# Single-token attention with a gated mixer branch: halved PE score sums, collects batched by four, the mixer moved to heads 22 to 24, and a fixed VectorE order

## The chip, the cores and the metric

The kernel runs on one core of one Trainium2 chip. The metric is the device time in microseconds (us). Engines are named as in the profile: PE is TensorE's matmul side, PEld its weight loads, DVE is VectorE, ACT is ScalarE, SP is SyncE, which here only issues DMA transfers.

Ratios are computed as the mean time of one kernel's runs over the mean of the other's runs in the same rounds, so a ratio is not quite the ratio of the medians quoted beside it.

## The reference, cut to what matters

```python
q = (x @ wq).reshape(1, 1, 32, 128)                 # one token, 32 heads of 128
scores = einsum(q, k_cache) * 128 ** -0.5           # k_cache: 32 heads x 16384 x 128, bf16
a = (softmax(scores) @ v_cache).reshape(1, 4096) @ wo
z = gelu(x @ w_in); z1, z2 = z[:896], layernorm(z[896:])
b = (z1 * (w_sp * z2 + b_sp)) @ w_out               # the mixer branch, on the same x
g = sigmoid((x * gate_w).sum())
out = g * a + (1 - g) * b                           # 512 numbers
```

The two caches are 32 heads x 2 x 4 MiB. With the weights they make 279.58 MB, of which every byte is read once and used for almost no arithmetic.

## The kernel before

Per head a k tile and a v tile of 128 x 16384 bf16 are loaded. DVE multiplies k by the broadcast q, in two halves. PE adds up slices of the product with an identity matrix as weights (16 matmuls of 512 columns per half), DVE reduces the 8 partial sums that are left, ACT takes the exponential. The attend uses 32 matmuls with four columns of p as weights, which leave their answer on the diagonal of a 4 x 4 block; ACT copies that out and 4 fp32 matmuls per head collect it.

```python
    def load_k(h):
        t = kv.tile([P, NJ * Dh], BF16, name="k_t", tag="k", bufs=3)
        nc.sync.dma_start(out=t[:], in_=k_src[h])
        ktile[h] = t
    # load_v(h): the same with tag "v", bufs=2
    load_k(0); load_k(1); load_k(2); load_v(0)
    # ... then the loads of w_in and w_out (the mixer's weights) ...

    def scores_half(h, s):
        # ... ks: half s of the k tile, qh: q broadcast over it ...
        nc.vector.tensor_tensor(out=ks, in0=ks, in1=qh, op=ALU.mult)
        s_ps = ps_s.tile([P, NH, W], FP32, name="s_ps")
        for i in range(NS):                       # NS = 16, W = 8
            nc.tensor.matmul(s_ps[:, :, :], lhsT=ident[:, :], rhs=ks[:, :, i * W:(i + 1) * W],
                             start=(i == 0), stop=(i == NS - 1))
        nc.vector.tensor_reduce(out=s_sb[:, s * NH:(s + 1) * NH], in_=s_ps[:, :, :],
                                axis=AX.X, op=ALU.add)
        # ... after the second half: the exponential, on ACT ...

    AHEAD = 2
    with tc.manual_schedule(engines={mybir.EngineType.PE}):   # PE in program order
        # ... scores of heads 0 and 1 ...
        for h in range(H - 1):
            if h > 0:
                # (only while h + AHEAD < H)
                load_k(h + AHEAD)
                load_v(h)
            scores_half(h + AHEAD, 0)
            if 0 < h <= WIDE:
                collect(h - 1)
            if h < WIDE:
                scores_half(h + AHEAD, 1)
                attend_wide(h)
            # ... else: the narrow attend of the last heads ...
            if h == 1:
                gate()
                mixer()          # z = x @ w_in, gelu, layernorm, u, then u @ w_out
```

A k buffer is free again when the sums of its head are done, a v buffer when its attend is done; only then can SP issue the next load into it (in the trace of the kernel before, SP waited 28 times for the matmuls of an attend before a v load, 333.0 us in all).

The softmax here doesn't subtract the row's maximum and nothing guards it: scores larger than these inputs give would overflow.

## Time and profile before

| | before |
|---|---|
| time, median of the first 4 runs | 662.51 us (661.65 to 663.8) |
| span of the profiled run | 662.0 us |
| DMA bytes; share of 16 engines' span | 279.58 MB; 98.5% |
| PE / DVE / ACT busy | 528.9 / 329.8 / 39.5 us |
| rate from 160 to 620 us | 424 to 440 GB/s |

The next lines are from the page of the kernel before: busy times with shares of the span and instruction counts; the DMA queues with packets, MB and share of 16 engines; and two groups of instructions (busy us, mean ns of one | idle time before them and what ended it).

```profile
span 662.0 us, 6195 instructions
PE 528.9 (80%) x2835; PEld 233.8 (35%) x2835; DVE 329.8 (50%) x164; ACT 39.5 (6%) x108; POOL 0.7 (0%) x6
...
q1 hardware_dynamic: 10520, 279.58, 98.5%
q8 instruction: 22, 0.36, 0.2%
...
L222 DVE TENSOR_TENSOR k_t<-k_t,qb 128x8192 bf16<-128x8192 bf16 x64 | 280.5, 4421 | 136.7 <-DMA k_t<-in_A_k_cache_dram 136.7
L225 PE MATMUL s_ps<-k_t,ident 128*128 128x512 bf16 x1024 | 268.9, 423 | 95.0 <-DVE k_t L222 95.0
```

The SP queue, q1, keeps the DMA engines busy 98.5% of the span, and DVE waits 136.7 us in all for k tiles to land: the kernel is limited by its loads, and PE's 80% is not a limit.

The table of stretches shows where the loads are not at their full rate. Its last two columns are the mean busy share of the DMA engines and GB/s.

```profile
120.00:124.00 4.00, 4.00 (x20) 1.61 (x19) 4.00 (x2) 1.69 (x3) 0.00 (x0) 1.00 0.93 401
124.00:128.00 4.00, 4.00 (x20) 1.54 (x18) 4.00 (x2) 0.57 (x1) 0.00 (x0) 1.00 0.58 213
128.00:132.00 4.00, 4.00 (x24) 2.17 (x22) 1.94 (x2) 0.00 (x0) 0.00 (x0) 1.00 0.85 344
132.00:136.00 4.00, 4.00 (x20) 1.63 (x19) 1.01 (x2) 0.29 (x2) 0.00 (x0) 1.00 1.02 442
```

The timeline of SP (start us, us, what) shows the cause, and that of DVE and PE what lies behind it:

```profile
92.11 0.33 SPq L85 DMA_DIRECT2D v_t<-in_A_v_cache_dram  x1
92.54 0.37 SPq L78 DMA_DIRECT2D k_t<-in_A_k_cache_dram  x1
126.89 0.33 SPq L85 DMA_DIRECT2D v_t<-in_A_v_cache_dram  x1
127.31 0.38 SPq L78 DMA_DIRECT2D k_t<-in_A_k_cache_dram  x1
...
98.83 4.42 DVE L222 TENSOR_TENSOR k_t<-k_t,qb 128x8192 bf16<-128x8192 bf16 x1
...
108.70 0.89 PE L207 MATMUL a_ps<-u,w_out 128*128 128x1 bf16 x28 [10.37 <-DVE u L202]
```

No load is issued from 92.5 to 126.9 us. PE, whose order is fixed, stands at the mixer's last matmul and waits 10.37 us for u, which DVE finishes late because two products of 4.4 us were put among the mixer's small steps. So the attend that frees the v buffer comes late, and the queue runs dry.

### The profile page before, as it was taken

How to read it: one execution, taken by the hardware profiler on the slowest of the kernel's cores; microseconds unless marked ns; L12 is line 12 of the kernel's file. 1: busy time of each engine (PE TensorE's matmuls, PEld its weight loads, DVE VectorE, ACT ScalarE, POOL GpSimd, SP SyncE). 2: the span in 40 equal slices, each digit the busy share in tenths (PEclk: the TensorE clock that was granted, in tenths of full speed). 3: DMA queues.
4: the chain of work that ended last, by engine and by line, in shares of the span. 5: the costliest groups of instructions: out<-in, count | busy, mean ns of one | idle time of the engine just before them, and what ended most of it. 6: DMA issues, size and time to landing. Idle time of an engine off the chain costs nothing.

```text
span 662.0 us, 6195 instructions
## 1 busy us (share of the span) xinstructions
PE 528.9 (80%) x2835; PEld 233.8 (35%) x2835; DVE 329.8 (50%) x164; ACT 39.5 (6%) x108; POOL 0.7 (0%) x6
## 2 busy tenths in 40 slices
PE   2777584999879798788799878789878879987884
PEld 0233242444323343333233333234333323333453
DVE  1592515666554445555444556444555544455600
ACT  0200020100000000000000000000000000000000
POOL 0000000000000000000000000000000000000000
PEclk9799595999989989889998988998988999897965
DMA  9999999899999999999999999999999999999995
GB/s 380 436 419 442 422 439 429 356 429 440 427 428 439 422 437 436 423 438 427 432 437 420 437 436 423 438 429 430 435 424 436 433 428 435 432 431 430 431 414 248
DMA packets 10554, 279.98 MB, mean 423 GB/s; under 512 B 1182, under 2 KB 1184, under 8 KB 1568
## 3 DMA queue, kind: packets, MB, share of 16 engines
q1 hardware_dynamic: 10520, 279.58, 98.5%
q8 instruction: 22, 0.36, 0.2%
q14 instruction: 4, 0.03, 0.0%
q10 hardware_dynamic: 8, 0.00, 0.0%
HBM read 279.58 MB, written 0.00 MB: 422 GB/s over the span
## 4 chain that ended last, share of the span: by engine, by line
DMA 60%; PE 30%; DVE 9%; SPq 1%; issue 0%; ACT 0%; DVEq 0%
DMA k_t<-in_A_k_cache_dram 52%; PE s_ps L225 15%; PE d_ps L250 12%; DVE k_t L222 8%; DMA v_t<-in_A_v_cache_dram 4%; DMA wo_t<-in_A_wo_dram 4%; PE o_ps L259 2%; SPq L85 1%; PE o_ps L239 1%; PE z_ps L167 0%; PE a_ps L317 0%; PE a_ps L207 0%; SPq L293 0%; PE tot_ps L184 0%; SPq L69 0%
## 5 line engine op out<-in xcount | busy, mean ns | idle before, releaser
L222 DVE TENSOR_TENSOR k_t<-k_t,qb 128x8192 bf16<-128x8192 bf16 x64 | 280.5, 4421 | 136.7 <-DMA k_t<-in_A_k_cache_dram 136.7
L225 PE MATMUL s_ps<-k_t,ident 128*128 128x512 bf16 x1024 | 268.9, 423 | 95.0 <-DVE k_t L222 95.0
L250 PE MATMUL d_ps<-v_t,p_t 128*4 128x512 bf16 x928 | 205.0, 379 | 0.0
L225 PEld LDWEIGHTS <-ident 128*128 128x128 bf16 x1024 | 105.9, 106 | 243.7 <-issue 148.2
L250 PEld LDWEIGHTS <-p_t 128*4 128x4 bf16 x928 | 76.4, 85 | 126.1 <-issue 12.3
L227 DVE TENSOR_REDUCE s_sb<-s_ps 128x64 f32<-128x512 f32 x64 | 44.2, 690 | 148.4 <-PE s_ps L225 148.4
L231 ACT ACTIVATE p_t<-s_sb 128x128 bf16<-128x128 f32 x32 | 9.9, 309 | 385.4 <-DVE s_sb L227 385.4
L259 PEld LDWEIGHTS o_ps<-ident_f,d_sb 4*128 4x128 f32 x232 | 27.9, 186 | 12.3 <-issue 12.3
L259 PE MATMUL o_ps<-ident_f,d_sb 4*128 4x1 f32 x232 | 30.4, 248 | 0.0
L254 ACT COPY d_sb<-d_ps 4x512 f32<-4x512 f32 x29 | 16.7, 575 | 170.7 <-PE d_ps L250 170.7
L121 PE MATMUL q_ps<-wq_t,xb 128*128 128x512 bf16 x32 | 9.7, 477 | 10.5 <-DMA wq_t<-in_A_wq_dram 10.5
L239 PE MATMUL o_ps<-p_t,v_t 128*128 128x1 bf16 x384 | 10.8, 165 | 4.4 <-DMA v_t<-in_A_v_cache_dram 4.3
L239 PEld LDWEIGHTS <-v_t 128*128 128x128 bf16 x384 | 10.5, 102 | 4.7 <-DMA v_t<-in_A_v_cache_dram 4.7
L121 PEld LDWEIGHTS <-xb 128*128 128x128 bf16 x32 | 3.7, 117 | 16.2 <-issue 13.1
L207 PE MATMUL a_ps<-u,w_out 128*128 128x1 bf16 x28 | 0.9, 165 | 10.4 <-DVE u L202 10.4
L317 PE MATMUL a_ps<-o,wo_t 128*128 128x1 bf16 x128 | 3.9, 166 | 4.2 <-DMA wo_t<-in_A_wo_dram 4.2
L124 DVE CAST qb<-q_ps 128x512 bf16<-128x512 f32 x1 | 0.7, 693 | 11.2 <-PE q_ps L121 11.2
L231 ACT ACTIVATION_READ_ACCUMULATOR p_t<-s_sb 128x1 f32 x32 | 6.0, 186 | 0.0
L304 DVE TENSOR_TENSOR o_sb<-o_ps,rl 128x32 bf16<-128x32 f32 x1 | 0.2, 192 | 10.3 <-PE o_ps L239 10.3
L317 PEld LDWEIGHTS <-wo_t 128*128 128x128 bf16 x128 | 3.6, 104 | 4.5 <-DMA wo_t<-in_A_wo_dram 4.5
L126 ACT CAST qb<-q_ps 128x512 bf16<-128x512 f32 x7 | 4.1, 586 | 15.9 <-PE q_ps L121 15.9
L207 PEld LDWEIGHTS <-w_out 128*128 128x128 bf16 x28 | 1.1, 111 | 10.4 <-issue 10.4
(65 smaller groups left out, 24.9 us busy)
## 6 DMA issues: line engine op xcount, KB each, us to landing
k_t<-in_A_k_cache_dram SPq DMA_DIRECT2D x32, 4096.0 KB, 37.5
v_t<-in_A_v_cache_dram SPq DMA_DIRECT2D x31, 4096.0 KB, 28.9
wq_t<-in_A_wq_dram SPq DMA_DIRECT2D x1, 4096.0 KB, 12.3
v_t<-in_A_v_cache_dram SPq DMA_DIRECT2D x1, 2048.0 KB, 11.1
v_t<-in_A_v_cache_dram SPq DMA_DIRECT2D x2, 1024.0 KB, 14.7
wo_t<-in_A_wo_dram SPq DMA_DIRECT2D x1, 2048.0 KB, 21.1
w_in<-in_B_w_in_dram SPq DMA_DIRECT2D x1, 1792.0 KB, 44.6
wo_t<-in_A_wo_dram SPq DMA_DIRECT2D x1, 1024.0 KB
```

Source lines behind the costliest of these rows:

```text
L85: nc.sync.dma_start(out=t[:, a * Dh:b * Dh], in_=v_src[h][:, a * Dh:b * Dh])
L121: nc.tensor.matmul(q_ps[:, :], lhsT=xb[:, c, :], rhs=wq[:, c, nb * QB:(nb + 1) * QB], start=(c == 0), stop=(c == DC - 1))
L126: nc.scalar.copy(out=qb[:, nb * QB:(nb + 1) * QB], in_=q_ps[:, :])
L222: nc.vector.tensor_tensor(out=ks, in0=ks, in1=qh, op=ALU.mult)
L225: nc.tensor.matmul(s_ps[:, :, :], lhsT=ident[:, :], rhs=ks[:, :, i * W:(i + 1) * W], start=(i == 0), stop=(i == NS - 1))
L227: nc.vector.tensor_reduce(out=s_sb[:, s * NH:(s + 1) * NH], in_=s_ps[:, :, :], axis=AX.X, op=ALU.add)
L231: nc.scalar.activation(out=p_t[:], in_=s_sb[:], func=ACT.Exp, scale=inv_sqrt_dh, accum_out=L_sb[:, h:h + 1])
L239: nc.tensor.matmul(o_ps[:, h:h + 1], lhsT=v3[:, j, :], rhs=p_sb[h][:, j:j + 1], start=(j == 0), stop=(j == NJ - 1))
L250: nc.tensor.matmul(d_ps[:, :], lhsT=p_sb[h][:, g * R:(g + 1) * R], rhs=vtile[h][:, g * R * Dh:(g + 1) * R * Dh], start=(g == 0), stop=(g = ...
L254: nc.scalar.copy(out=d_sb[:], in_=d_ps[:, :])
L259: nc.tensor.matmul(o_ps[:, h:h + 1], lhsT=diag[h][:, r * Dh:(r + 1) * Dh], rhs=ident_f[:, r:r + 1], start=(r == 0), stop=(r == R - 1))
L317: nc.tensor.matmul(a_ps[:, c:c + 1], lhsT=wo4[:, k, c, :], rhs=o2[:, k:k + 1], start=False, stop=(k == H - 1), skip_group_check=True)
```

## The change

Its intent is to take work off PE and to take the mixer out of the critical start. Four things change: (1) from head 3 DVE adds the upper half of each product to the lower one, in bf16, so PE sums 8 slices per half; (2) four heads' attends share one PSUM bank (rows 0, 32, 64, 96), which is drained and collected once; (3) the mixer's loads are issued at head 19 and its work is cut into pieces placed at heads 22 to 24; (4) the order of DVE is fixed too. The gate's sum is taken on 8 partitions by DVE, with one small matmul over them, instead of by eight matmuls.

```diff
-    NS = Dh // W
+    NS = Dh // 2 // W
@@ loads of w_in, w_out, gate_w, w_sp, b_sp: from the start into load_mixer(), called at h == MIX - 3 @@
+    def scores_mult(h):
+        # ... qh as before ...
+        for ks in halves(h):
+            nc.vector.tensor_tensor(out=ks, in0=ks, in1=qh, op=ALU.mult)
+            if h > 2:
+                nc.vector.tensor_tensor(out=ks[:, :, 0:Dh // 2], in0=ks[:, :, 0:Dh // 2],
+                                        in1=ks[:, :, Dh // 2:Dh], op=ALU.add)
+    def scores_sum(h, s):
+        # ...
+        ns = NS if h > 2 else 2 * NS
+    # scores_exp(h): both reduces, then the exponential
@@ attend and collect @@
+    G = 4
-        d_ps = ps_s.tile([R, R * Dh], FP32, name="d_ps")
+        d_ps = d_banks[(h // G) % 2]
+            nc.tensor.matmul(d_ps[32 * g:32 * g + R, :], lhsT=p_sb[h][:, t * R:(t + 1) * R], ...
+                if h % G == G - 1 or h == WIDE - 1:
+                    drain(h - h % G)
+                    due = (h - h % G, h % G + 1)
@@ the loop @@
-    with tc.manual_schedule(engines={mybir.EngineType.PE}):
+    MIX = 22
+    dve_extra = {MIX: [gate_x], MIX + 1: [gate_out, mixer_gelu], MIX + 2: [mixer_norm]}
+    pe_extra = {MIX: [gate_ps, mixer_z], MIX + 1: [mixer_tot], MIX + 2: [mixer_out]}
+    with tc.manual_schedule(engines={mybir.EngineType.PE, mybir.EngineType.DVE}):
-            if h == 1:
-                gate()
-                mixer()
```

More of the change, by code (lines that the diff above doesn't have):

```diff
@@ L60 @@
     x_row = const.tile([1, D], BF16, name="x_row")
-    gw_row = const.tile([1, D], BF16, name="gw_row")
-    wb_row = const.tile([1, 2], BF16, name="wb_row")
     nc.scalar.dma_start(out=x_row[:], in_=A_x.rearrange("b s d -> (b s) d"))
-    nc.scalar.dma_start(out=gw_row[:], in_=gate_w.rearrange("(a d) -> a d", a=1))
-    nc.scalar.dma_start(out=wb_row[:, 0:1], in_=B_w_sp)
-    nc.scalar.dma_start(out=wb_row[:, 1:2], in_=B_b_sp.rearrange("(a d) -> a d", a=1))
     wq_t = kv.tile([P, DC * HDh], BF16, name="wq_t", tag="v")
@@ L100 @@
     load_v(0)
-    w_in = const.tile([P, DC, F], BF16, name="w_in")
-    nc.sync.dma_start(out=w_in[:].rearrange("p c f -> p (c f)"),
-                      in_=B_w_in.rearrange("(p c) f -> p (c f)", c=DC))
-    w_out = const.tile([P, FhC, D], BF16, name="w_out")
-    nc.sync.dma_start(out=w_out[:].rearrange("p k n -> p (k n)"),
-                      in_=B_w_out.rearrange("(p k) n -> p (k n)", k=FhC))
     xb_ps = ps_m.tile([P, DC * P], FP32, name="xb_ps", tag="mm")
@@ L132 @@
                               in_=ident[0:H, 0:H])
-    ident_f = const.tile([4, 4], FP32, name="ident_f")
-    nc.vector.tensor_copy(out=ident_f[:], in_=ident[0:4, 0:4])
+    pick = const.tile([P, 4, 4], FP32, name="pick")
+    nc.vector.tensor_copy(out=pick[:].rearrange("p r g -> p g r"),
+                          in_=ident[:].rearrange("p (g m) -> p g m", m=32)[:, :, 0:4])
+    d_banks = [ps_1.tile([P, 512], FP32, name=f"d_ps{i}") for i in range(2)]
+    for t in d_banks:
+        nc.vector.memset(t[:, :], 0.0)
     a_ps = ps_1.tile([P, 512], FP32, name="a_ps")
@@ L141 @@
     wbf = const.tile([P, 2], FP32, name="wbf")
-    def gate():
-        gw_ps = ps_m.tile([P, DC + 2], FP32, name="gw_ps", tag="mm")
-        for c in range(DC):
-            nc.tensor.matmul(gw_ps[:, c:c + 1], lhsT=gw_row[0:1, c::DC], rhs=ones_row[0:1, 0:1],
-                             start=True, stop=True)
-        nc.tensor.matmul(gw_ps[:, DC:DC + 2], lhsT=ones_row[0:1, :], rhs=wb_row[0:1, :],
-                         start=True, stop=True)
-        gw_col = const.tile([P, DC], BF16, name="gw_col")
-        nc.vector.tensor_copy(out=gw_col[:], in_=gw_ps[:, 0:DC])
-        nc.vector.tensor_copy(out=wbf[:], in_=gw_ps[:, DC:DC + 2])
-        g_ps = ps_m.tile([P, 1], FP32, name="g_ps", tag="mm")
-        for c in range(DC):
-            nc.tensor.matmul(g_ps[:, :], lhsT=xb[:, c, :], rhs=gw_col[:, c:c + 1],
-                             start=(c == 0), stop=(c == DC - 1))
-        nc.scalar.activation(out=g_sb[:], in_=g_ps[:, :], func=ACT.Sigmoid)
-        nc.scalar.activation(out=gm_sb[:], in_=g_ps[:, :], func=ACT.Sigmoid, scale=-1.0)
@@ L162, in mixer, with load_mixer @@
-    def mixer():
+    w_in = const.tile([P, DC, F], BF16, name="w_in")
+    w_out = const.tile([P, FhC, D], BF16, name="w_out")
+    xg = const.tile([8, 2, D // 8], BF16, name="xg")
+    wb_row = const.tile([1, 2], BF16, name="wb_row")
+    def load_mixer():
+        nc.sync.dma_start(out=w_in[:].rearrange("p c f -> p (c f)"),
+                          in_=B_w_in.rearrange("(p c) f -> p (c f)", c=DC))
+        nc.sync.dma_start(out=xg[:, 0, :], in_=A_x.rearrange("b s (p d) -> (b s p) d", p=8))
+        nc.sync.dma_start(out=xg[:, 1, :], in_=gate_w.rearrange("(p d) -> p d", p=8))
+        nc.sync.dma_start(out=wb_row[:, 0:1], in_=B_w_sp)
+        nc.sync.dma_start(out=wb_row[:, 1:2], in_=B_b_sp.rearrange("(a d) -> a d", a=1))
+        nc.sync.dma_start(out=w_out[:].rearrange("p k n -> p (k n)"),
+                          in_=B_w_out.rearrange("(p k) n -> p (k n)", k=FhC))
@@ new lines, with gate_x, gate_ps @@
+    branch = {}
+    def gate_x():
+        xgp = const.tile([8, D // 8], BF16, name="xgp")
+        nc.vector.tensor_mul(out=xgp[:], in0=xg[:, 0, :], in1=xg[:, 1, :])
+        xgs = const.tile([8, 1], FP32, name="xgs")
+        nc.vector.reduce_sum(out=xgs[:], in_=xgp[:], axis=AX.X)
+        branch["xgs"] = xgs
+    def gate_ps():
+        xgs = branch["xgs"]
+        g_ps = ps_m.tile([P, 3], FP32, name="g_ps", tag="mm")
+        nc.tensor.matmul(g_ps[:, 0:1], lhsT=ones_f[0:8, :], rhs=xgs[:, :], start=True, stop=True)
+        nc.tensor.matmul(g_ps[:, 1:3], lhsT=ones_row[0:1, :], rhs=wb_row[0:1, :],
+                         start=True, stop=True)
+        branch["g_ps"] = g_ps
@@ L163, in mixer, with gate_out, mixer_z @@
+    def gate_out():
+        g_ps = branch["g_ps"]
+        nc.vector.tensor_copy(out=wbf[:], in_=g_ps[:, 1:3])
+        nc.scalar.activation(out=g_sb[:], in_=g_ps[:, 0:1], func=ACT.Sigmoid)
+        nc.scalar.activation(out=gm_sb[:], in_=g_ps[:, 0:1], func=ACT.Sigmoid, scale=-1.0)
+    z = const.tile([P, FC], FP32, name="z")
+    stats = const.tile([P, 2], FP32, name="stats")
+    u = const.tile([P, FhC], BF16, name="u")
+    def mixer_z():
         z_ps = ps_m.tile([P, FC], FP32, name="z_ps", tag="mm")
@@ L168, in mixer, with mixer_gelu @@
                                  rhs=xb[:, c, 0:1], start=(c == 0), stop=(c == DC - 1))
-        z = const.tile([P, FC], FP32, name="z")
-        nc.vector.tensor_copy(out=z[:], in_=z_ps[:])
+        branch["z_ps"] = z_ps
+    def mixer_gelu():
+        nc.vector.tensor_copy(out=z[:], in_=branch["z_ps"][:])
         t = const.tile([P, FC], FP32, name="t")
@@ L177, in mixer @@
         nc.vector.tensor_mul(out=z[:], in0=z[:], in1=t[:])
-        stats = const.tile([P, 2], FP32, name="stats")
         nc.vector.reduce_sum(out=stats[:, 0:1], in_=z[:, FhC:FC], axis=AX.X)
@@ L182, in mixer, with mixer_tot, mixer_norm @@
         nc.vector.reduce_sum(out=stats[:, 1:2], in_=sq[:], axis=AX.X)
+    def mixer_tot():
         tot_ps = ps_m.tile([P, 2], FP32, name="tot_ps", tag="mm")
         nc.tensor.matmul(tot_ps[:, :], lhsT=ones_f[:, :], rhs=stats[:, :], start=True, stop=True)
+        branch["tot"] = tot_ps
+    def mixer_norm():
+        tot_ps = branch["tot"]
         mv = const.tile([P, 2], FP32, name="mv")
@@ L200, in mixer, with mixer_out @@
         nc.vector.tensor_mul(out=uf[:], in0=z[:, 0:FhC], in1=z2n[:])
-        u = const.tile([P, FhC], BF16, name="u")
         nc.vector.tensor_scalar(out=u[:], in0=uf[:], scalar1=gm_sb[:, 0:1], scalar2=0.0,
                                 op0=ALU.mult, op1=ALU.add)
+    def mixer_out():
         w_out4 = w_out[:].rearrange("p k (c m) -> p k c m", c=DC)
@@ L211, with halves, scores_exp @@
     p_sb = {}
-    s_tile = {}
-    def scores_half(h, s):
+    s_part = {}
+    def halves(h):
         k3 = ktile[h][:].rearrange("p (j d) -> p j d", d=Dh)
+        return [k3[:, s * NH:(s + 1) * NH, :] for s in range(2)]
+    def scores_mult(h):
         qh = qb[:, h * Dh:(h + 1) * Dh].unsqueeze(1).broadcast_to([P, NH, Dh])
-        if s == 0:
-            s_tile[h] = sp.tile([P, NJ], FP32, name="s_sb")
-        s_sb = s_tile[h]
-        ks = k3[:, s * NH:(s + 1) * NH, :]
-        nc.vector.tensor_tensor(out=ks, in0=ks, in1=qh, op=ALU.mult)
+        for ks in halves(h):
[4 more added lines that the diff above has]
+    def scores_sum(h, s):
+        ks = halves(h)[s]
         s_ps = ps_s.tile([P, NH, W], FP32, name="s_ps")
-        for i in range(NS):
+        ns = NS if h > 2 else 2 * NS
+        for i in range(ns):
             nc.tensor.matmul(s_ps[:, :, :], lhsT=ident[:, :], rhs=ks[:, :, i * W:(i + 1) * W],
-                             start=(i == 0), stop=(i == NS - 1))
-        nc.vector.tensor_reduce(out=s_sb[:, s * NH:(s + 1) * NH], in_=s_ps[:, :, :],
-                                axis=AX.X, op=ALU.add)
-        if s == 1:
-            p_t = sp.tile([P, NJ], BF16, name="p_t", bufs=4)
-            nc.scalar.activation(out=p_t[:], in_=s_sb[:], func=ACT.Exp, scale=inv_sqrt_dh,
-                                 accum_out=L_sb[:, h:h + 1])
-            p_sb[h] = p_t
+                             start=(i == 0), stop=(i == ns - 1))
+        s_part[h, s] = s_ps
+    def scores_exp(h):
+        s_sb = sp.tile([P, NJ], FP32, name="s_sb")
+        for s in range(2):
+            nc.vector.tensor_reduce(out=s_sb[:, s * NH:(s + 1) * NH], in_=s_part[h, s][:, :, :],
+                                    axis=AX.X, op=ALU.add)
+        p_t = sp.tile([P, NJ], BF16, name="p_t", bufs=4)
+        nc.scalar.activation(out=p_t[:], in_=s_sb[:], func=ACT.Exp, scale=inv_sqrt_dh,
+                             accum_out=L_sb[:, h:h + 1])
+        p_sb[h] = p_t
     def attend(h):
@@ L243 @@
     R = 512 // Dh
+    G = 4
     diag = {}
     def attend_wide(h):
-        d_ps = ps_s.tile([R, R * Dh], FP32, name="d_ps")
+        g = h % G
+        d_ps = d_banks[(h // G) % 2]
         NG = NJ // R
-        for g in range(NG):
-            nc.tensor.matmul(d_ps[:, :], lhsT=p_sb[h][:, g * R:(g + 1) * R],
-                             rhs=vtile[h][:, g * R * Dh:(g + 1) * R * Dh],
-                             start=(g == 0), stop=(g == NG - 1))
-        d_sb = sp.tile([R, R * Dh], FP32, name="d_sb")
@@ L254, in attend_wide, with drain @@
-        nc.scalar.copy(out=d_sb[:], in_=d_ps[:, :])
-        diag[h] = d_sb
-    def collect(h):
+        for t in range(NG):
+            nc.tensor.matmul(d_ps[32 * g:32 * g + R, :], lhsT=p_sb[h][:, t * R:(t + 1) * R],
+                             rhs=vtile[h][:, t * R * Dh:(t + 1) * R * Dh],
+                             start=(t == 0), stop=(t == NG - 1))
+    def drain(h0):
+        d_sb = sp.tile([P, R * Dh], FP32, name="d_sb", bufs=1)
+        nc.scalar.copy(out=d_sb[:], in_=d_banks[(h0 // G) % 2][:, :])
+        diag[h0] = d_sb
@@ L258, in collect @@
+    def collect(h0, n):
         for r in range(R):
-            nc.tensor.matmul(o_ps[:, h:h + 1], lhsT=diag[h][:, r * Dh:(r + 1) * Dh],
-                             rhs=ident_f[:, r:r + 1], start=(r == 0), stop=(r == R - 1))
+            nc.tensor.matmul(o_ps[:, h0:h0 + n], lhsT=diag[h0][:, r * Dh:(r + 1) * Dh],
+                             rhs=pick[:, r, 0:n], start=(r == 0), stop=(r == R - 1))
     AHEAD = 2
     WIDE = H - 3
-    with tc.manual_schedule(engines={mybir.EngineType.PE}):
+    MIX = 22
@@ L265 @@
+    dve_extra = {MIX: [gate_x], MIX + 1: [gate_out, mixer_gelu], MIX + 2: [mixer_norm]}
+    pe_extra = {MIX: [gate_ps, mixer_z], MIX + 1: [mixer_tot], MIX + 2: [mixer_out]}
+    due = None
+    with tc.manual_schedule(engines={mybir.EngineType.PE, mybir.EngineType.DVE}):
         for h in range(AHEAD):
-            scores_half(h, 0)
-            scores_half(h, 1)
+            scores_mult(h)
+            scores_sum(h, 0)
+            scores_sum(h, 1)
+            scores_exp(h)
         for h in range(H - 1):
+            ahead = h + AHEAD if h + AHEAD < H else None
@@ L269 @@
             if h > 0:
-                if h + AHEAD < H:
-                    load_k(h + AHEAD)
+                if ahead is not None:
+                    load_k(ahead)
                 load_v(h)
-            if h + AHEAD < H:
-                scores_half(h + AHEAD, 0)
-            if 0 < h <= WIDE:
-                collect(h - 1)
+            if h == MIX - 3:
+                load_mixer()
+            if ahead is not None:
+                scores_mult(ahead)
+            for f in dve_extra.get(h, ()):
+                f()
@@ L277 @@
+            if ahead is not None:
+                scores_sum(ahead, 0)
+            if due is not None:
+                collect(*due)
+                due = None
             if h < WIDE:
-                scores_half(h + AHEAD, 1)
+                scores_sum(ahead, 1)
                 attend_wide(h)
+                if h % G == G - 1 or h == WIDE - 1:
+                    drain(h - h % G)
+                    due = (h - h % G, h % G + 1)
             else:
                 attend(h)
-                if h + AHEAD < H:
-                    scores_half(h + AHEAD, 1)
@@ L284 @@
-            if h == 1:
-                gate()
-                mixer()
+                if ahead is not None:
+                    scores_sum(ahead, 1)
+            if ahead is not None:
+                scores_exp(ahead)
+            for f in pe_extra.get(h, ()):
+                f()
         load_v(H - 1, cuts=(64, 96))
```

## The prediction

> **What bounds it now.** The DMA stream. The page's queue table gives the SP queue 279.58 MB and 98.5% of the 16 DMA engines' span; the table of 20 us windows shows 424 to 440 GB/s in every window from 160 to 620 us, about 431 on average. [...] 280 MB at 431 GB/s is 650 of the 662.0 us. PE (529 us busy) and DVE (330) have slack: of a head's 19.4 us (8.39 MB at 431), it needs 8.8 us of DVE products, 1.4 of reduces, about 7.1 of PE sums and 7.0 of wide attends. In steady state each v load is issued some 29 us before it lands.
>
> **Where DMA is not full.** Start and end: first bytes after 1.5 us, last weights near 658, then 4 us of small work. Otherwise one hole: 120 to 132 us moves 401, 213 and 344 GB/s, short of 431 by about 3.2 us of transfer. The SP timeline shows why: k and v loads are issued at 92 us, the next only at 127. The mixer at head 1 sits in PE's order between them: PE waits 10.4 us for u, and the next head's product starts at 98.8.
>
> **What the change does.**
> - Bytes are the same but for 1 KB. Four tiny loads join the SP queue: under 0.5 us.
> - The mixer's loads go to head 19, its work to heads 22 to 24, with a full queue ahead. The hole should go: -3 us, all critical, as nothing later makes up for it.
> - PE: 16 sum matmuls per half become 8 from head 3: 464 x about 0.23 us off; collects once in four heads (30 us busy to about a quarter). PE falls to about 390 us. Critical: 0.
> - DVE: 58 bf16 additions of 4096 elements. The product's 8192 take 4.42 us, so 2.2 to 2.3 us each by scaling: +130 us, DVE to about 460. [...] A head is then 13.4 us of products and additions, 1.4 of reduces and, with DVE order fixed, about 2.3 waiting for PE's second half: about 17 us, under 19.4. Critical: 0, but DVE is now close.
> - Start: head 1's product waits for head 0's last reduce (about +4 us), and 2.75 MB less is queued. I estimate v2 issued near 74 us with the queue lasting to about 80: no hole.
> - The mixer's DVE work, about 3 and 4 us with ACT waits, fits the issue margin (15 us).
>
> **Time.** 662.5 - 3 + 0.3: about 659.8 us, range 657.3 to 663.3. Faster by over 2%: 0.02; within 2%: 0.93; slower by over 2%: 0.05.
>
> **What shows it.** SP queue near 99% of the span; no 20 us window under 400 GB/s between 20 and 640 us; no 35 us gap in the issues near 92; PE busy near 390, DVE near 460; additions at 2.2 to 2.3 us; DVE still waiting for k transfers at most heads; the tail after the last weights unchanged at 4 us.
>
> **What would make it wrong.** [...] A hole near 80 us because PE is slow after its early idle time: up to +3. A stall of the in-order DVE at heads 22 to 24 beyond the margin. [...]

Passages on the hardware that no trace or run of this case shows are cut where marked: a ceiling on the DMA rate (that the rate could not rise was not shown), a limit on the speed of the additions, and two of the risks. The sum: 662.5 - 3 for the hole + 0.3 = 659.8 us. The 0.3, and the "under 0.5 us" for the four tiny loads, are estimates; in the trace of the changed kernel their data packets took 0.23 us in all. The 2.2 to 2.3 us are an estimate too, half of the 4.42 us that the trace of the kernel before gives for a product of twice as many elements. That PE is slow after its early idle time can be read in the same trace: after 10.23 us of idle time the 16 sums at 74.05 us took 6.49 us at a granted clock of 0.55, and the 16 at 81.45 us took 3.63 us at 1.00.

## The result, and the profile after

| | before | after |
|---|---|---|
| median, all runs beside each other | 662.58 us (15 runs) | 660.48 us (10 runs) |
| ratio, 95% interval | | 0.9966, 0.9957 to 0.9975 |
| same kernel again, later | 662.63 us (11 runs) | 659.94 us (6 runs), ratio 0.9958, 0.9945 to 0.9971 |
| span of the profiled run | 662.0 us | 658.8 us |
| PE / DVE / ACT busy | 528.9 / 329.8 / 39.5 us | 449.3 / 462.5 / 28.2 us |

The change is worth 2.1 to 2.7 us by medians, a third to four tenths of a per cent. The profiled run of the kernel before took 663.80 us, the most of its 15 runs, so the two spans and traces lie further apart (3.2 us) than the medians do. These are the lines of the page of the changed kernel that answer to those above (line numbers have moved):

```profile
span 658.8 us, 4965 instructions
PE 449.3 (68%) x2197; PEld 179.0 (27%) x2197; DVE 462.5 (70%) x225; ACT 28.2 (4%) x88; POOL 0.7 (0%) x6
...
q1 hardware_dynamic: 10556, 279.58, 99.0%
q8 instruction: 17, 0.28, 0.2%
...
L247 DVE TENSOR_TENSOR k_t<-k_t,qb 128x8192 bf16<-128x8192 bf16 x64 | 282.7, 4422 | 64.0 <-DMA k_t<-in_A_k_cache_dram 64.0
L257 PE MATMUL s_ps<-k_t,ident 128*128 128x512 bf16 x560 | 193.1, 510 | 183.2 <-DVE k_t L249 168.2
...
L249 DVE TENSOR_TENSOR k_t<-k_t 128x4096 bf16<-128x4096 bf16 x58 | 132.9, 2292 | 2.0
```

The additions take 2292 ns each. DVE still waits for k at most heads, but 64.0 us in all instead of 136.7. PE has a little over half of its sum matmuls left (560 of 1024), yet each now takes 510 ns instead of 423.

The stretches around the old hole, and the issues in it, in the changed kernel:

```profile
120.00:140.00 20.00, 14.59 (x65) 6.06 (x63) 14.64 (x6) 1.29 (x5) 0.00 (x0) 0.91 1.03 442
140.00:160.00 20.00, 14.18 (x51) 4.96 (x49) 14.66 (x7) 0.40 (x2) 0.00 (x0) 0.83 0.98 421
...
89.31 0.33 SPq L80 DMA_DIRECT2D v_t<-in_A_v_cache_dram  x1
...
106.48 0.33 SPq L80 DMA_DIRECT2D v_t<-in_A_v_cache_dram  x1
...
126.51 0.33 SPq L80 DMA_DIRECT2D v_t<-in_A_v_cache_dram  x1
```

The hole is gone: 442 and 421 GB/s, and an issue every 17 to 20 us. To see more than windows show, I added up the bytes of all DMA packets in the trace and asked how far each kernel is behind a steady 431 GB/s (us):

```
at us        20    120    140    300    500    620    640    651
before      2.5    2.5    5.3    5.2    5.2    5.2    5.3    5.5
after       2.4    2.3    2.4    2.4    2.7    2.7    3.5    3.7
```

The kernel before loses 2.8 us in the hole and nothing else until the end. The changed one loses nothing there, then some 0.6 us near 622 us, where only one v load was queued for a moment. These are means over the 16 engines.

So far the prediction seems right in every part. It was not: the experiments show that two of its terms were wrong and, by luck, nearly cancelled.

### The profile page after: what moved, and what is told of

It reads as the page before. It is cut to its first block, busy times and chain, and to the rows that moved or that the text cites. A ratio compares the mean times of both kernels' runs of the same rounds, so it can differ in the third digit from the quotient of the medians.

```text
span 658.8 us, 4965 instructions
## 1 busy us (share of the span) xinstructions
PE 449.3 (68%) x2197; PEld 179.0 (27%) x2197; DVE 462.5 (70%) x225; ACT 28.2 (4%) x88; POOL 0.7 (0%) x6
## 4 chain that ended last, share of the span: by engine, by line
DMA 55%; DVE 23%; PE 20%; SPq 1%; issue 0%; DVEq 0%
DMA k_t<-in_A_k_cache_dram 44%; DVE k_t L247 15%; PE d_ps L289 10%; PE s_ps L257 9%; DVE k_t L249 7%; DMA w_in<-in_B_w_in_dram 4%; DMA v_t<-in_A_v_cache_dram 4%; DMA wo_t<-in_A_wo_dram 4%; SPq L80 1%; PE o_ps L275 1%; DVE s_sb L264 0%; PE a_ps L376 0%; SPq L352 0%; SPq L64 0%; PE rT_ps L381 0%
## 5 line engine op out<-in xcount | busy, mean ns | idle before, releaser
L257 PE MATMUL s_ps<-k_t,ident 128*128 128x512 bf16 x560 | 193.1, 510 | 183.2 <-DVE k_t L249 168.2
L289 PE MATMUL d_ps<-v_t,p_t 128*4 128x512 bf16 x928 | 219.8, 398 | 0.0
L257 PEld LDWEIGHTS <-ident 128*128 128x128 bf16 x560 | 67.6, 121 | 294.2 <-issue 265.1
L249 DVE TENSOR_TENSOR k_t<-k_t 128x4096 bf16<-128x4096 bf16 x58 | 132.9, 2292 | 2.0
L289 PEld LDWEIGHTS <-p_t 128*4 128x4 bf16 x928 | 79.1, 88 | 148.8 <-issue 45.1
L295 ACT COPY d_sb<-d_ps 128x512 f32<-128x512 f32 x8 | 4.7, 586 | 172.1 <-PE d_ps L289 172.1
L300 PEld LDWEIGHTS o_ps<-pick,d_sb 128*128 128x128 f32 x64 | 10.7, 237 | 1.8 <-issue 0.8
L300 PE MATMUL o_ps<-pick,d_sb 128*128 128x4 f32 (+1 forms) x64 | 9.5, 272 | 0.0
(66 smaller groups left out, 28.2 us busy)
## 6 DMA issues: line engine op xcount, KB each, us to landing
wo_t<-in_A_wo_dram SPq DMA_DIRECT2D x1, 2048.0 KB, 20.5
```

Source lines behind the costliest of these rows:

```text
L249: nc.vector.tensor_tensor(out=ks[:, :, 0:Dh // 2], in0=ks[:, :, 0:Dh // 2], in1=ks[:, :, Dh // 2:Dh], op=ALU.add)
L289: nc.tensor.matmul(d_ps[32 * g:32 * g + R, :], lhsT=p_sb[h][:, t * R:(t + 1) * R], rhs=vtile[h][:, t * R * Dh:(t + 1) * R * Dh], start=(t ...
L295: nc.scalar.copy(out=d_sb[:], in_=d_banks[(h0 // G) % 2][:, :])
L300: nc.tensor.matmul(o_ps[:, h0:h0 + n], lhsT=diag[h0][:, r * Dh:(r + 1) * Dh], rhs=pick[:, r, 0:n], start=(r == 0), stop=(r == R - 1))
```

## The experiments

Theory H: the change gains by removing the hole, and by that alone. Rival P: it gains by the PE (and ACT) work that it takes away. Rival L: it gains because 2.75 MB are no longer loaded at the start. Later theory F was added: PE's instructions themselves are fetched over the same DMA engines (the 22 packets of q8 in the kernel before), and this costs time. Each kernel ran five rounds beside the kernel before on the same chip, except that half_only has four runs. Executions over 1.5% slower than the fastest of the same kernel are left out of the means.

| run | what it is | median us | ratio, 95% interval | PE instructions | fetch packets |
|---|---|---|---|---|---|
| late_work | before, mixer's work at head 22 | 660.97 | 0.9984, 0.9971 to 0.9996 | 5670 | 22 |
| no_half | after, without the additions | 661.40 | 0.9989, 0.9976 to 1.0001 | 5322 | 21 |
| early_spread | after, mixer at heads 1 to 3 | 660.44 | 0.9972, 0.9958 to 0.9986 | 4394 | 17 |
| half_only | before, with the additions alone | 707.03 | 1.0681, 1.0661 to 1.0700 | 4742 | 18 |
| auto_dve | after, DVE order left to the scheduler | 675.97 | 1.0187, 1.0155 to 1.0219 | 4394 | 17 |
| collect_each | after, a collect per head | 661.31 | 0.9982, 0.9968 to 0.9995 | 4730 | 18 |
| more_instr | after, 1856 tiny matmuls added | 663.37 | 1.0015, 1.0001 to 1.0028 | 8106 | 31 |
| loads_only | before, loads without the work | 657.58 | 0.9925, 0.9913 to 0.9937 | 852 | 3 |
| after_again | after | 659.94 | 0.9958, 0.9945 to 0.9971 | 4394 | 17 |
| more_busy | after, 232 large matmuls added | 661.27 | 0.9977, 0.9964 to 0.9990 | 4829 | 19 |
| quarter | after, a second addition | 660.84 | 0.9971, 0.9959 to 0.9984 | 3930 | 15 |
| dve_plus | after, one addition twice | 668.33 | 1.0083, 1.0069 to 1.0096 | 4394 | 17 |

All gave the correct result but loads_only. The PE instructions are the matmuls and weight loads that the pages record (PE and PEld; a few can be missing), the fetch packets are those of line q8. On this count the kernel before has 5670 and 22, the changed one 4394 and 17. (The 4267, 7979 and 464 of some expectations come from a count in the programs; the pages have 4394 and 8106.)

### late_work: the hole alone

```diff
-            if h == 1:
+            if h == 22:
                 gate()
                 mixer()
```

> The kernel before with one line changed: gate and mixer are called at head 22 instead of head 1, in one piece; their loads stay at the start, nothing else changes. Theory H (the change gains only by removing the DMA hole at 120 to 132 us): the hole there is gone and the time falls by 2 to 3 us, to about 660; the one-piece mixer may open a smaller hole after head 22, which would show as a window under 400 GB/s near 520 us and take up to 1 us back. Rival P (the gain comes from the PE and ACT work removed by halving and batching): 662.5, no change. Rival L (the gain comes from taking 2.75 MB out of the start): 662.5.

Measured: 660.97 against 662.28 us, and by the ratio 1.1 us faster (0.3 to 1.9 by its interval), not 2 to 3. The hole at 120 us is gone (437 and 428 GB/s in the windows from 80 to 120, 435 from 120 to 140). A smaller one opens after head 22 (344 GB/s from 532 to 536 us). So lateness does cure the first hole, as H said, but it is worth about a third of what I had put on it.

```profile
120.00:140.00 20.00, 17.40 (x84) 7.62 (x82) 10.05 (x4) 0.98 (x3) 0.00 (x0) 1.00 1.01 435
532.00:536.00 4.00, 4.00 (x20) 1.64 (x19) 3.38 (x1) 0.58 (x1) 0.00 (x0) 1.00 0.90 344
```

To see why, I laid the packets of the kernel before end to end into 16 chains, one per DMA engine; the trace as I have it does not name a packet's engine, so this is a reconstruction. In the hole the 16 chains stand idle for

```
0.45 0.60 0.65 1.99 2.15 2.20 2.29 2.36 2.50 2.60 2.67 2.94 3.07 3.19 3.43 3.57   us
```

The mean is 2.3 us, but the engine that was furthest behind idled only 0.45 us. Its loss is larger than its idle time: the last packet before the hole ends at 127.38 us, and the next packet of every engine ends between 129.57 and 130.10 us, after 1.2 to 2.2 us instead of the usual 1.2. Whichever chain it is, that engine lost 1.0 to 1.5 us, about what late_work measures, where the sum of bytes lost 2.8. The k load that ended before the hole landed at 127.8 us, just after that last packet: it landed when its slowest engine had done its part. What counts for the end here is what the slowest engines lose, not the mean over engines that the windows show. In late_work's second hole, by the same reconstruction, 11 of the 16 chains stop for 0.1 us or not at all. The size of 1.1 us rests on the timed runs: the two profiled runs, 663.80 and 660.97 us, lie 2.8 us apart.

### early_spread: early, but in pieces

```diff
-    MIX = 22
+    MIX = 1
+    load_mixer()
```

> The changed kernel with the mixer early: its loads right after the first v load and its work at heads 1 to 3, but still in pieces with the fixed order on DVE and PE. Theory H in the form that the hole came from the mixer blocking PE's order in one piece: no gap of 35 us between issues and no hole, 660 to 661, as the changed kernel. In the form that lateness alone (a full queue) cures it: a hole of 2 to 3 us between 80 and 140 us and about 662.5.

Measured: 660.44 us, like the changed kernel; v loads are issued at 71.7, 93.3 and 111.1 us, with no gap of 35 us. So the move to head 22 is not needed: cut into pieces with a fixed order, the mixer does no harm at heads 1 to 3 either. This also rules out rival L, as the 2.75 MB are back at the start.

### no_half: everything but the halving

```diff
         for ks in halves(h):
             nc.vector.tensor_tensor(out=ks, in0=ks, in1=qh, op=ALU.mult)
-            if h > 2:
-                nc.vector.tensor_tensor(...)            # the addition
-        ns = NS if h > 2 else 2 * NS
+        ns = 2 * NS
```

> The changed kernel without the halving additions: DVE makes the products only and PE sums 16 slices per half at every head, as before. Mixer late, order of DVE fixed, collects batched, as in the changed kernel. Theory H: no loss, and as DVE no longer takes 18.3 of 19.4 us per head, the v loads are issued some 4 us earlier and the thin queue near 620 us fills again: 659.5 to 660.5, equal to the changed kernel or up to 0.8 us faster. Rival P: back towards 662.5, as PE has its 270 us of sums again.

Measured: 661.40 us. It was expected to be equal or faster than the changed kernel, and it is 1.0 us slower than early_spread in the same rounds; the slowest early_spread run (660.62) is faster than the fastest no_half run (661.31). The dip near 622 us did vanish, as I had expected: by 640 us the sum of bytes is 0.4 us ahead of the changed kernel's. It did not help; by the reconstruction 9 of the changed kernel's 16 chains do not stop in the dip, so it idles engines that are ahead. So H does not hold alone: about half of the gain goes when the halving goes, although PE keeps up with the loads in no_half too (DVE waits 5.47 and 6.29 us for k before the heads at 199 and 218 us).

### half_only: the halving without the rest

```diff
         nc.vector.tensor_tensor(out=ks, in0=ks, in1=qh, op=ALU.mult)
+        if h > 2:
+            nc.vector.tensor_tensor(out=ks[:, :, 0:Dh // 2], in0=ks[:, :, 0:Dh // 2],
+                                    in1=ks[:, :, Dh // 2:Dh], op=ALU.add)
+        ns = NS // 2 if h > 2 else NS
```

> The kernel before with the halving alone: from head 3 an addition of 4096 elements after each product and 8 sums per half. The mixer stays in one piece at head 1. Theory H: the hole at 120 to 132 us stays (perhaps 1 us smaller or larger, as PE catches up sooner but DVE later), time 661.5 to 663.5, PE busy down by 60 to 80 us, DVE up by 133. Rival P: about 660.5, the whole gain.

Measured: 707.03 us, 45 us slower; neither theory had this. DVE's timeline for one head (207.01 to 227.55 us):

```profile
207.01 8.75 DVE L222 TENSOR_TENSOR k_t<-k_t,qb 128x8192 bf16<-128x8192 bf16 x2
215.68 4.49 DVE L224 TENSOR_TENSOR k_t<-k_t 128x4096 bf16<-128x4096 bf16 x2
221.69 0.69 DVE L231 TENSOR_REDUCE s_sb<-s_ps 128x64 f32<-128x512 f32 x1 [1.53 <-PE s_ps L229]
226.94 0.69 DVE L231 TENSOR_REDUCE s_sb<-s_ps 128x64 f32<-128x512 f32 x1 [4.56 <-PE s_ps L229]
227.55 4.42 DVE L222 TENSOR_TENSOR k_t<-k_t,qb 128x8192 bf16<-128x8192 bf16 x1
```

The scheduler put both products ahead of both additions, so the sums of both halves come together at the end, with the head's collect between them, and DVE waits 1.53 and 4.56 us. A head takes 20.5 us of DVE and PE in turn, over the 19.4 us in which its 8.39 MB arrive at 431 GB/s. The kernel is then limited by that loop, head after head. Compare the changed kernel, from the same view:

```profile
198.94 4.42 DVE L247 TENSOR_TENSOR k_t<-k_t,qb 128x8192 bf16<-128x8192 bf16 x1 [1.76 <-DMA k_t<-in_A_k_cache_dram]
203.40 2.29 DVE L249 TENSOR_TENSOR k_t<-k_t 128x4096 bf16<-128x4096 bf16 x1
205.61 4.42 DVE L247 TENSOR_TENSOR k_t<-k_t,qb 128x8192 bf16<-128x8192 bf16 x1
210.06 2.29 DVE L249 TENSOR_TENSOR k_t<-k_t 128x4096 bf16<-128x4096 bf16 x1
212.27 0.69 DVE L264 TENSOR_REDUCE s_sb<-s_ps 128x64 f32<-128x512 f32 x1
216.01 0.69 DVE L264 TENSOR_REDUCE s_sb<-s_ps 128x64 f32<-128x512 f32 x1 [3.05 <-PE s_ps L257]
218.31 4.43 DVE L247 TENSOR_TENSOR k_t<-k_t,qb 128x8192 bf16<-128x8192 bf16 x1 [1.61 <-DMA k_t<-in_A_k_cache_dram]
```

Here the first half's sums run under the second half's product. A head takes 17.8 us (198.94 to 216.70), and DVE then waits 1.61 us for the next k: the loads are the limit again.

### auto_dve and collect_each: which part keeps the halving harmless

```diff
 auto_dve
-    with tc.manual_schedule(engines={mybir.EngineType.PE, mybir.EngineType.DVE}):
+    with tc.manual_schedule(engines={mybir.EngineType.PE}):
 collect_each
-    G = 4
+    G = 1
```

> The changed kernel with only PE's order fixed; the scheduler orders DVE, and puts both products of a head before both additions, as it did in half_only (20.5 us per head, against 19.4 of loads; 17.8 in the changed kernel). Theory O (the fixed DVE order is what keeps the halving off the critical path): a head costs 20.5 less the 1.9 us of a collect in three heads of four, so 18.7 to 19.3 us, at the edge: 660.5 to 666. If the batched collect alone were enough: 660.5 exactly, with DVE still waiting for k over 1 us a head. If order does it all: near 700.

> The changed kernel with a drain and collect for every head (group size 1 in place of 4). Theory O: with the fixed order the collect of 1 to 2 us hides behind the second addition, a head stays at 17.8 us: 660 to 661.5, PE busy up some 20 us. Rival (batching is what keeps halving off the critical path): about 19.7 us a head and 670 or more.

Measured: collect_each 661.31 us, so with a fixed DVE order the collect of every head hides from DVE, as theory O said. It is still 0.8 to 1.4 us over the two medians of the changed kernel, as much as no_half: without the batching, too, about half of the gain is gone. The section on more_instr shows why. auto_dve 675.97 us (671.45 to 677.69): outside the 660.5 to 666 that I expected, and the reason is partly another one. At most heads DVE still waits for k (2.27 us before the head at 199 us), so pairing the products is just bearable when the collects are batched. More than half of the loss is at the mixer, where the scheduler made DVE wait for PE before it started the next product:

```profile
496.44 0.69 DVE L264 TENSOR_REDUCE s_sb<-s_ps 128x64 f32<-128x512 f32 x1 [1.67 <-PE s_ps L257]
503.78 0.16 DVE L171 COPY wbf<-g_ps 128x2 f32<-128x2 f32 x1 [6.65 <-PE g_ps L165]
506.85 0.17 DVE L189 COPY z<-z_ps 128x14 f32<-128x14 f32 x1 [2.91 <-PE z_ps L184]
...
508.48 4.42 DVE L247 TENSOR_TENSOR k_t<-k_t,qb 128x8192 bf16<-128x8192 bf16 x1
```

Because of these waits the next product starts 11.4 us after the last reduce; a wait of 6.62 us for tot_ps follows at the next head, and then 303 and 327 GB/s in the windows from 540 to 580 us. The rest is lost in the last heads: 347 and 345 GB/s from 620 to 660 us, after windows in which DVE is as busy as in dve_plus below (16.9 and 17.1 of 20 us). No run took that apart. In the changed kernel the same small steps stand behind the additions, in time that DVE would have spent waiting for the second half's sums. The fixed order is thus a condition of the halving, not a detail.

### loads_only: the floor

```diff
-        nc.vector.tensor_tensor(out=ks, in0=ks, in1=qh, op=ALU.mult)      # and sums, reduces, collect (cut short)
+        nc.vector.tensor_copy(out=L_sb[:, h:h + 1], in_=ktile[h][:, 0:1])  # one element per row
-        for j in range(NJ):                                               # attend
+        for j in range(NJ if h == H - 1 else 1):
-                attend_wide(h)
+                attend(h)
-            if h == 1:
+            if h == 22:
```

> Wrong result on purpose: the kernel before with the same loads in the same order, but the products, sums and wide attends taken out (one element of each k tile read, one matmul per v tile; the last attend and the tail kept). The floor of this list of loads. Theory H with the skew of engines: few instructions, so few fetch packets and 656 to 659; if the changed kernel is within 0.5% of this, nothing is left but the loads. If something other than the loads bounds the changed kernel: under 650.

Measured: 657.58 us, with a wrong result. This is what the list of loads costs with almost no work. The changed kernel is 2.4 to 2.9 us above it (0.4%): there is nearly nothing left to gain but bytes.

### more_instr and more_busy: what the halving saves

```diff
 more_instr, at the end of attend_wide
+        for t in range(64):
+            nc.tensor.matmul(x_ps[:, 0:1], lhsT=ident[:, :], rhs=ident[:, t:t + 1], start=True, stop=True)
 more_busy, in the same place
+        for t in range(8):
+            nc.tensor.matmul(x_ps[:, :], lhsT=ident[:, :], rhs=qb[:, 0:512], start=True, stop=True)
```

> The changed kernel with 64 extra matmuls of one column per wide head on PE (1856 in all, results unused, nothing waits for them): PE goes from 4267 to 7979 instructions, its busy time from 449 to some 500 us, still under that of the kernel before. Theory F (the instruction fetch packets of 16 KB go through the same DMA engines and delay the slowest of them, so fewer PE instructions save time): fetch packets go from 17 to some 31, the last weights land later by 1 to 2 us, time 661.5 to 662.5. Theory H alone: 660.5, as no wait on the critical path changes.

> The changed kernel with 8 extra matmuls of 512 columns per wide head on PE (232 in all, results unused), in the place where more_instr had 64 of one column: about as much extra PE time (50 us) for an eighth of the instructions (464 more, 2 more fetch packets). Theory F (more_instr lost its 3 us to instruction fetch): 660.5 to 661.3. Rival B (it lost them to PE's extra 1.75 us per head, which delays the v loads): 663 to 664.

> The changed kernel itself, as the partner of the three runs beside it on the same chip: 660.0 to 661.0.

Measured: more_instr 663.37 us, 2.9 to 3.4 us over the two medians of the changed kernel, more than either theory had; PE busy 496.7 us. more_busy 661.27 us, PE busy 486.2 us: 1.3 us over after_again in the same rounds, at the upper edge of what F allowed and far from the 663 to 664 of rival B. Most of more_instr's loss therefore goes with the number of instructions, not with PE's time; the landings below leave nothing for PE's time. The page of more_instr:

```profile
span 661.7 us, 8679 instructions
...
q8 instruction: 31, 0.51, 0.3%
```

Every q8 packet has 16384 bytes, and their number goes with that of the PE instructions: 17 packets for 4394 in the changed kernel and 31 for 8106 in more_instr, one for every 258 and 261. A packet occupies a DMA engine for 1.0 to 1.1 us: in the middle of each of the changed kernel's packets but the last, 15 packets of data are under way, where it is mostly 16 otherwise. For comparison, a whole 4 MiB load is 128 packets of 32768 bytes and 1.2 us, 8 for each of the 16 engines.

The load of w_in gives a clean reading of what this does. It stands at the same place of the queue in all variants of the changed kernel that keep the mixer late, and its first packet starts at 420.2 to 420.4 us in each of those listed (in dve_plus, left out, at 423.4). Its last packet ends when the slowest engine gets there:

```
run            fetch packets before it ended   first start to last end of w_in   time, median
quarter         7 (of 15)                       6.9 us                            660.84
after           8 (of 17)                       6.4                               660.48
after_again     8 (of 17)                       6.3                               659.94
auto_dve        8 (of 17)                       6.6                               (other cause)
collect_each    9 (of 18)                       7.6                               661.31
more_busy       9 (of 19)                       7.5                               661.27
no_half        11 (of 21)                       7.7                               661.40
more_instr     18 (of 31)                       9.3                               663.37
```

Up to 8 packets it takes 6.3 to 6.9 us, at 9 to 11 it takes 7.5 to 7.7, at 18 it takes 9.3: steps of one packet's length and a little more, at multiples of eight. That is what one would see if the fetches went to eight of the 16 engines in turn, so that the ninth puts a second packet on one of them. The eight engines are an inference (the durations of no_half's fetch packets also repeat with period eight); the steps are measured. The times follow: about 660.2 us with two full rounds of eight before the end (the changed kernel's 17th packet comes at 653.9 us), 661.3 to 661.4 with a third begun, 663.4 with a fourth. quarter does not fit, and is taken up below.

The times at which whole loads land (issue plus time to landing) say the same without any reconstruction. Undisturbed, a 4 MiB load lands every 9.72 us in both kernels, so the added work on DVE does not slow the loads. Measured against that pace, each run falls behind in steps (us behind before and after the step, and the packet's number and start):

```
after         1st (49.7)  3.3 to 4.4    9th (450.3)  4.9 to 6.0
no_half       1st (49.7)  3.1 to 4.6    9th (347.7)  4.6 to 5.9    17th (629.2)  6.3 to 8.0
more_busy     1st (49.8)  3.2 to 4.5    9th (391.6)  4.7 to 6.0    17th (640.7)  6.4 to 7.8
collect_each  1st (49.9)  3.2 to 4.6    9th (397.8)  4.6 to 6.1    17th (646.1)  6.6 to 8.0
more_instr    1st (50.0)  3.2 to 4.6    9th (227.7)  4.7 to 6.1    17th (404.3)  6.2 to 7.8    25th (569.1)  7.8 to 9.3
```

Between these steps the runs drift by 0.5 us at most up to 616 us. From there to about 647 us, past the dip, the changed kernel and more_instr both fall 0.8 us back. The two further steps of more_instr, 3.1 us, are its whole loss: a v load that lands at 605.5 us in the changed kernel lands at 608.7 there, and the last weights with a recorded landing 2.9 us later (657.8 against 654.9). So the loss is there before the dip near 622 us, and PE's time need not be called on. The further step of more_busy, no_half and collect_each at their 17th packet, 1.3 to 1.7 us, is about what each of them loses. The table rests on one profiled run of each.

### quarter and dve_plus: how much room DVE has

```diff
 quarter, after the first addition (and 4 sums per half)
+                nc.vector.tensor_tensor(out=ks[:, :, 0:Dh // 4], in0=ks[:, :, 0:Dh // 4],
+                                        in1=ks[:, :, Dh // 4:Dh // 2], op=ALU.add)
 dve_plus, in the first half only
+                    nc.vector.tensor_tensor(out=ks[:, :, Dh // 2:Dh], in0=ks[:, :, 0:Dh // 2],
+                                            in1=ks[:, :, Dh // 2:Dh], op=ALU.add)
```

> The changed kernel with a second addition per half (2048 elements, some 1.2 us by scaling from 2.29 and 4.42), so 4 sums per half: PE has 464 instructions fewer (two fetch packets less). A head on DVE: 17.8 plus 2.4, less about 1.7 of the wait for PE's second half, so 18.5 us, still under 19.4. Theory F: 0.3 to 0.6 us faster than the changed kernel in the same rounds, 659.9 to 660.3. If the head is longer than that and crosses 19.4: 665 or more.

> The changed kernel with one more addition of 4096 elements per head from head 3 on (2.29 us; its result is not used): measures how close DVE is to the limit. By the trace a head takes 17.8 us of DVE, so 20.1 against 19.4 to 19.5 of loads: 0.6 us over per head, 18 us over the 29 heads, of which the queue hides up to 12: 663 to 680, and DVE waits for k in the first heads only. If a head were 17.1, as predicted before the result: no change, 660.5.

Measured: dve_plus 668.33 us, in the range worked out from the trace. A head is then 20.0 us of DVE with no wait for k between heads, and the loss shows at the end, when no more queued loads cover it (287 GB/s from 620 to 640 us):

```profile
194.34 4.42 DVE L247 TENSOR_TENSOR k_t<-k_t,qb 128x8192 bf16<-128x8192 bf16 x1
198.80 2.29 DVE L249 TENSOR_TENSOR k_t<-k_t 128x4096 bf16<-128x4096 bf16 x1
...
204.75 0.69 DVE L267 TENSOR_REDUCE s_sb<-s_ps 128x64 f32<-128x512 f32 x1 [3.06 <-PE s_ps L260]
...
214.34 4.42 DVE L247 TENSOR_TENSOR k_t<-k_t,qb 128x8192 bf16<-128x8192 bf16 x1
```

So the changed kernel stands 1.6 us per head from this limit.

quarter, meant as a version that beats both, missed: 660.84 us, 0.9 us slower than after_again in the same rounds, although it has two fetch packets fewer and a head (18.6 us at 199 us) stays under 19.4. Its v loads land 22.2 us after issue (median of all), against 24.4 in the changed kernel and 27.2 in the one before, and near 622 us its bytes fall 1.0 us behind, against 0.4 in after_again. Its landings agree: 0.2 us ahead of after_again's at 606 us, 0.8 behind at 646. So a thin queue is the likely cause. No run took that apart; it stays open. No version tried is faster than the changed kernel.

## Why the prediction was right or wrong

The predicted time (659.8 us) and range (657.3 to 663.3) held, with 660.48 and 659.94 us measured. Point by point:

- "What bounds it now. The DMA stream": right. loads_only takes 657.58 us.
- "The hole should go: -3 us, all critical, as nothing later makes up for it": the mechanism was right, the size wrong. The hole went, but removing it alone is worth 1.1 us by late_work's ratio and 0.7 by no_half's (that interval reaches 1.0001). The hole was sized by the mean over 16 engines; the engine furthest behind lost 1.0 to 1.5 us in it.
- "PE falls to about 390 us. Critical: 0": wrong twice. PE fell to 449.3, because its matmuls became slower (510 ns from 423, with the granted clock at 0.822 instead of 0.903). In the trace of the changed kernel PE was busy for 17% of the 3 us before a spell at a granted clock of 0.50, on average, and for 99% of the 3 us before a return to 1.00. And the fewer instructions are worth about 1.0 us (early_spread against no_half), which the prediction did not have at all. So two errors, of about 2 us and 1 us in opposite directions, left the total nearly right: the number held by luck.
- "DVE: 58 bf16 additions ... 2.2 to 2.3 us each", "DVE to about 460": right, 2.29 us and 462.5.
- "about 17 us, under 19.4": a little short. A head takes 17.8, because the second half's sums run at the low clock (8 sums take 3.56 us from 212.41 us, at a granted clock of 0.52, where the first half's 8 took 1.89 at 1.00; so a wait of 3.05 us, not 2.3). dve_plus shows that 20.0 us costs 8 us.
- "v2 issued near 74 us with the queue lasting to about 80: no hole": right; it was issued at 71.2.
- "The mixer's DVE work ... fits the issue margin": right, and early_spread shows the margin was not needed. What was needed, and what the prediction took for granted, is the fixed order: without it the kernel takes 675.97 us.

What stays open: why quarter is slower than the changed kernel, and the last heads of auto_dve. The chain reconstruction and the eight engines are inferences; the steps at every eighth packet are measured.

## What to carry to other kernels

In a kernel limited by its loads, size a gap in the DMA by the engine that is furthest behind, not by the mean share that the windows show: here the sum of bytes lost 2.8 us in the hole, that engine 1.0 to 1.5 us by the reconstruction, and late_work, without the hole, was 1.1 us faster by its ratio. Instructions are loads too: here, with the DMA engines at 99.0% of the span, 3712 more PE instructions cost about 3 us, on engines that no wait in the profile names. And an engine that gets new work off the critical path should be given its order as well: with its order left to the scheduler the same kernel took 15 us longer.
